# A 2D-DFT mixing layer and a SoLU feed-forward layer: even and odd halves shared between two frequencies, and the transposition of u by 32 x 32 blocks and moves

## The chip, the cores and the metric

The kernel runs on one core of a Trainium2 chip, in one launch. The metric is the device time of that launch in microseconds (us); the kernel before takes 2172.12 us, the median of 3 runs (2170.49 to 2173.72). The engines are called by the names of the profile: PE (matrix multiply), PEld (its weight loads), DVE (vector), ACT (scalar, activation functions), POOL (GpSimd), SP (which issues transfers), and the 16 DMA engines.

## What is computed

The reference takes x of 8 batches x 3136 rows x 256 features and does two layers:

```python
X = np.fft.fft(np.fft.fft(x, axis=1), axis=2).real      # (8, 3136, 256)
h = X.reshape(25088, 256) @ w_in                        # (25088, 1024)
e = np.exp(h - h.max(-1)); sm = e / (e.sum(-1) + 1e-9)
solu = h * sm
ln = (solu - mean(solu)) / np.sqrt(var(solu) + 1e-6) * g_ln
out = ln @ w_out                                        # (25088, 256)
```

All data are float32 to the kernel, except that the weights can come as float64 words, which it narrows itself.

## The kernel before

**First part, the transform over the sequence.** The 3136 positions are 49 x 64. Batches are taken in four pairs. `load` brings in rows and their mirror rows, `fold` adds x[n, d] and x[-n, -d] on POOL (L121) and forms sums and differences over the features on DVE (L112, L113), `transform1` sums over 49 with matmuls (L148), ACT evicts (L151), the result goes through DRAM (`zd`) and `turn` brings it back with another index on the partitions. `transform2` (L166) sums over 64. Only 25 of the 49 residues k1 are computed: for each k1 the product gives the "+" frequency, and with the sign of half of the features changed the "-" frequency. The feature transform is folded into w_in beforehand, so it costs nothing per token.

**Second part.** For each pair, k1 and sign there is one tile of 128 tokens, 4 x 49 = 196 tiles in all. On a tile:

- `up_half`, twice: h, a 128 x 1024 tile in PSUM, from two 128 x 128 stationary blocks of q (or qm, its copy with the changed sign, made at L176) against `Wi` (L190).
- `solu`: the maximum of h (L195, DVE), the exponential with its sum (L198, ACT), u = h * e with its sum (L200, DVE), the mean on POOL (L203), the centred square with its sum (L206, ACT), and five small POOL operations for the reciprocal root.
- `transpose`: eight PE transposes of u (L224) into PSUM, evicted half by ACT (L230) and half by DVE (L228).
- `down`: eight matmuls of 128 x 256 (L235) against `Wo`, scaled by DVE (L237) and stored. The layer norm's scale and mean lie in `Wo`.

**Order.** The program's order is written out by hand: for tile i, the first half of up(i), transpose(i-1), the second half of up(i), solu(i), then (on a "+" tile) transform2 of the next k1 and one step of the next pair's first part, and last down(i-1). `ahead` spreads a pair's first part over the 25 steps of the pair before it; the first pair's runs alone at the start, followed by the preparation of the weights. The PSUM pools are `ps_h` (2 tiles of 2 banks), `ps_t` (2 banks) and `ps_m` (2 banks, shared by the results of transform1, transform2 and down).

Of the kernel before, what the change touches and what calls it, by code (L numbers as in the profile page):

```python
# [10 lines left out]
I32 = mybir.dt.int32  # L11
ALU = mybir.AluOpType
# [5 lines left out]
# The sequence index is n = N2 * n1 + n2 and its frequency k = k1 + N1 * k2.  # L18
# The frequencies k1 of 0..NK-1 are computed; k1 and N1 - k1 share their products.
# [5 lines left out]
CH = 8  # L25
NC = NH // CH

# The layout of the 256 folded features: cosine part at 0..128, sine part (1..127) at 129..255.
# [4 lines left out]
def kernel(  # L33
# [13 lines left out]
    """Sequence DFT with even and odd folds, feature DFT folded into w_in, then SoLU and its layer norm.  # L47

    With U the cosine transform over the sequence of x folded evenly in the features, and V the sine
    transform of x folded oddly, the real part of the 2D DFT is U C - V S at frequency k and U C + V S  # L50
    at -k. So h = [U, V] @ [C w_in; -S w_in], and for -k the features of V change their sign.
    """
# [10 lines left out]
    out_b = out.rearrange("(b s) d -> b s d", b=B)  # L63
# [4 lines left out]
    gpool = ctx.enter_context(tc.tile_pool(name="gpool", bufs=2))  # L68
    qpool = ctx.enter_context(tc.tile_pool(name="qpool", bufs=3))
    small = ctx.enter_context(tc.tile_pool(name="small", bufs=4))  # L70
    dram = ctx.enter_context(tc.tile_pool(name="dram", bufs=2, space=bass.MemoryType.DRAM))
    ps_h = ctx.enter_context(tc.tile_pool(name="ps_h", bufs=2, space=PSUM))
    ps_t = ctx.enter_context(tc.tile_pool(name="ps_t", bufs=2, space=PSUM))
    ps_m = ctx.enter_context(tc.tile_pool(name="ps_m", bufs=2, space=PSUM))

    F = const.tile([PR, 6, ZR], FP32, name="F")
    T = const.tile([P, NK, P], FP32, name="T")
    Wi = const.tile([P, KD, FF], FP32, name="Wi")
    Wo = const.tile([P, KF, D], FP32, name="Wo")
    ident = const.tile([P, P], FP32, name="ident")  # L80
    ones = const.tile([P, P], FP32, name="ones")
    neg_half = const.tile([P, 1], FP32, name="neg_half")
    idx = const.tile([PR, NP * NC], I32, name="idx")
    sg = const.tile([P, 1], FP32, name="sg")

# [1 line left out]

    class Pair:
        def __init__(self, p):
            self.p = p  # L90
            self.raw, self.y, self.y0 = {}, {}, None
            self.g = None

    def load(pr, c):
        """Rows n2 = 8c + 1 .. 8c + 8, and those of S - n beside them (in descending order of n2)."""
        r = slice(pr.p * PR, (pr.p + 1) * PR)
        xa = xpool.tile([PR, CH, D], FP32, tag="xa", name="xa")
        xb = xpool.tile([PR, CH, D], FP32, tag="xb", name="xb")
        nc.sync.dma_start(out=xa, in_=x_pn[r, c * CH + 1 : (c + 1) * CH + 1, :])
        i = pr.p * NC + c  # L100
        nc.gpsimd.indirect_dma_start(
            out=xb.rearrange("p l d -> p (l d)"), out_offset=None, in_=x_g,
            in_offset=bass.IndirectOffsetOnAxis(ap=idx[:, i : i + 1], axis=0))
        x0 = None
        if c == NC - 1:
            x0 = xpool.tile([PR, 1, D], FP32, tag="x0", name="x0", bufs=1)
            nc.sync.dma_start(out=x0, in_=x_pn[r, 0:1, :])
        pr.raw[c] = (xa, xb, x0)

    def fold_features(o, i):  # L110
# [3 lines left out]
        nc.vector.tensor_copy(out=o[:, :, 0:129:128], in_=i[:, :, 0:129:128])  # L114

    def fold(pr, c):
        """x[n, d] + x[-n, -d], then its even and odd parts in d. Rows n2 = 0 and 32 hold their own mirrors."""
        xa, xb, x0 = pr.raw.pop(c)
        n = CH - 1 if c == NC - 1 else CH
        a, rb = xa[:, 0:n, :], xb[:, ::-1, :][:, 0:n, :]  # L120
        nc.gpsimd.tensor_tensor(out=a[:, :, 1:D], in0=a[:, :, 1:D], in1=rb[:, :, D - 1 : 0 : -1], op=ALU.add)  # L121
        nc.gpsimd.tensor_tensor(out=a[:, :, 0:1], in0=a[:, :, 0:1], in1=rb[:, :, 0:1], op=ALU.add)
        y = xpool.tile([PR, CH, D], FP32, tag="y", name="y")
        fold_features(y, xa)
        pr.y[c] = y
        if c == NC - 1:
            pr.y0 = xpool.tile([PR, 1, D], FP32, tag="y0", name="y0", bufs=1)
            fold_features(pr.y0, x0)

    def transform1(pr, s):  # L130
        """Sum over n1 for rows n2 = 2s + 1, 2s + 2; out: (b, cosine or sine, k1) on partitions.

        The last row holds n2 = 0, of no sine part, in its cosine part and n2 = 32 in its sine part."""
# [3 lines left out]
        if l == 0:  # L137
            pr.z = zpool.tile([ZR, CH, D], FP32, tag="z", name="z")
# [13 lines left out]
        if l == CH - 2:  # L152
            nc.sync.dma_start(out=pr.zd[:, c * CH : (c + 1) * CH, :], in_=pr.z)

    def turn(pr):
        """(b, cosine or sine, n2) onto partitions."""
        pr.g = gpool.tile([P, NK, D], FP32, tag="g", name="g")
        for j in range(4):
            nc.sync.dma_start(out=pr.g[j * NH : (j + 1) * NH, :, :],
                              in_=pr.zd[j * NK : (j + 1) * NK, :, :].rearrange("k n d -> n k d"))  # L160

    def transform2(pr, k1):
        """Sum over n2 for both batches; out: folded features on partitions, tokens (b, k2) free."""
        ps = ps_m.tile([P, KD, P], FP32, tag="m", name="ps2")
        for h in range(KD):
            nc.tensor.matmul(ps[:, h, :], pr.g[:, k1, h * P : (h + 1) * P], T[:, k1, :],  # L166
                             start=(h == 0), stop=(h == KD - 1), skip_group_check=True)
        q = {"+": qpool.tile([P, KD, P], FP32, tag="q", name="q")}
        nc.vector.tensor_copy(out=q["+"], in_=ps)  # L169
        if k1:  # L170
            # -(k1 + 49 k2) is (49 - k1) + 49 (63 - k2): the negative frequencies run backwards.
            q["-"] = qpool.tile([P, KD, P], FP32, tag="qm", name="qm")
            for h in range(KD):
                o = q["-"][:, h, :].rearrange("p (b k) -> p b k", b=2)
                i = ps[:, h, :].rearrange("p (b k) -> p b k", b=2)[:, :, ::-1]
                nc.scalar.activation(out=o, in_=i, func=ACT.Copy, scale=sg if h else 1.0)  # L176
        return q

# [1 line left out]

    class Tokens:
        def __init__(self, p, k1, s):
            self.p, self.k1, self.s = p, k1, s

    def up_half(t, half):
        if half == 0:
            t.h = ps_h.tile([P, FF], FP32, tag="h", name="h")
        fs = slice(half * HW, (half + 1) * HW)
        for h in range(KD):
            nc.tensor.matmul(t.h[:, fs], t.q[:, h, :], Wi[:, h, fs], start=(h == 0), stop=(h == KD - 1))  # L190

    def solu(t):
        """u = h exp(h - max h), its sum and centred sum of squares, and the sum of the exponentials."""
        nmax = small.tile([P, 1], FP32, tag="nmax", name="nmax")
        nc.vector.tensor_reduce(out=nmax, in_=t.h, axis=AX.X, op=ALU.max, negate=True)  # L195
        t.u = fpool.tile([P, FF], FP32, tag="u", name="u")
        esum = small.tile([P, 1], FP32, tag="esum", name="esum")
        nc.scalar.activation(out=t.u, in_=t.h, func=ACT.Exp, bias=nmax, accum_out=esum)  # L198
        usum = small.tile([P, 1], FP32, tag="usum", name="usum")
        nc.vector.scalar_tensor_tensor(out=t.u, in0=t.h, scalar=1.0, in1=t.u, op0=ALU.mult, op1=ALU.mult,  # L200
                                       accum_out=usum)
        nmean = small.tile([P, 1], FP32, tag="nmean", name="nmean")
        nc.gpsimd.tensor_scalar(out=nmean, in0=usum, scalar1=-1.0 / FF, scalar2=None, op0=ALU.mult)  # L203
        sq = fpool.tile([P, FF], FP32, tag="sq", name="sq", bufs=1)
        ssq = small.tile([P, 1], FP32, tag="ssq", name="ssq")
        nc.scalar.activation(out=sq, in_=t.u, func=ACT.Square, bias=nmean, accum_out=ssq)  # L206
        # 1 / (sum * sqrt(var(u / sum) + 1e-6)) = (var(u) + 1e-6 sum^2) ** -0.5
        es = small.tile([P, 1], FP32, tag="es", name="es")
        nc.gpsimd.tensor_scalar(out=es, in0=esum, scalar1=1e-9, scalar2=1e-3, op0=ALU.add, op1=ALU.mult)
        es2 = small.tile([P, 1], FP32, tag="es2", name="es2")  # L210
        nc.gpsimd.tensor_tensor(out=es2, in0=es, in1=es, op=ALU.mult)
        v = small.tile([P, 1], FP32, tag="v", name="v")
        nc.gpsimd.tensor_scalar(out=v, in0=ssq, scalar1=1.0 / FF, scalar2=es2, op0=ALU.mult, op1=ALU.add)  # L213
# [237 lines left out]
```

## Time and profile before

| | busy us | share of the span |
|---|---|---|
| PE | 1788.7 | 83% |
| PEld | 1238.2 | 57% |
| DVE | 846.8 | 39% |
| ACT | 670.6 | 31% |
| POOL | 382.0 | 18% |

The profiled span is 2166.9 us with 19414 instructions; the mean granted clock of the PE is 0.903. A float32 matmul leaves two records: the 196 tiles x 4 matmuls of L190 are 1568 records. The ends of PE records are modelled, so durations of PE work are best read as differences between starts. The transfers average 39 GB/s over the span.

### The profile page before, as it was taken

To read this page: it belongs to the slowest core of one execution; us is meant where nothing else is said; L and a number is where in the kernel's file an instruction comes from. 1 tells how busy PE (TensorE), PEld (TensorE's weight loads), DVE (VectorE), ACT (ScalarE), POOL (GpSimd) and SP (SyncE) were. 2 spreads that over 40 slices of the span, in tenths; PEclk is the share of its full clock that TensorE was granted. 3 is DMA by queue.
4 is the path that set the end of the run, shared out by engine and by line. 5 is a ranking of instruction groups with operands and counts; after the bars stand their busy time and mean duration, and the time that the engine had idled before them with its cause. 6 is when DMAs were issued, how large, how long until landed. Compare 5 with 4: busy or idle time off the path is not lost. (4 is left out here: it accounts for less than half of the span.)

```text
span 2166.9 us, 19414 instructions
## 1 busy us (share of the span) xinstructions
PE 1788.7 (83%) x6992; PEld 1238.2 (57%) x6992; DVE 846.8 (39%) x1327; ACT 670.6 (31%) x1240; POOL 382.0 (18%) x1034
## 2 busy tenths in 40 slices
PE   2357888788799878878879987887887999999998
PEld 1135555555566555555556755555555666777666
DVE  2853233323334323332433433333233344444444
ACT  1113223223333322332332323233233234434443
POOL 3002121212112212121211221212121111111111
PEclk8679899889899888888999988889899899999999
DMA  9511010001042101000104210101010400000000
GB/s 240 133 33 42 24 46 13 25 13 28 10 90 75 42 20 50 12 26 12 28 11 88 77 42 16 54 10 28 11 29 11 88 18 18 17 16 18 18 18 17
DMA packets 56783, 84.78 MB, mean 39 GB/s; under 512 B 12038, under 2 KB 50574, under 8 KB 51696
## 3 DMA queue, kind: packets, MB, share of 16 engines
q1 hardware_dynamic: 48528, 65.19, 12.7%
q0 software_dynamic: 2048, 12.85, 2.1%
q10 hardware_dynamic: 6112, 5.52, 1.3%
q8 instruction: 55, 0.90, 0.2%
q14 instruction: 40, 0.33, 0.1%
HBM read 44.72 MB, written 38.80 MB: 39 GB/s over the span
## 5 line engine op out<-in xcount | busy, mean ns | idle before, releaser
L235 PE MATMUL ps_o<-Wo,uT 128*128 128x256 f32 x3136 | 833.5, 425 | 270.8 <-ACT qm L176 215.9
L235 PEld LDWEIGHTS ps_o<-Wo,uT 128*128 128x128 f32 x3136 | 668.7, 217 | 444.7 <-ACT qm L176 235.5
L198 ACT ACTIVATE u<-h,nmax 128x1024 f32<-128x1024 f32 x196 | 218.4, 1114 | 634.3 <-DVE nmax L195 634.3
L190 PE MATMUL h<-Wi,q 128*128 128x512 f32 x800 | 384.4, 604 | 7.8 <-DVE q L169 7.8
L190 PE MATMUL h<-Wi,qm 128*128 128x512 f32 x768 | 361.1, 592 | 0.0
L200 DVE SCALAR_TENSOR_TENSOR u<-h,u 128x1024 f32<-128x1024 f32 x196 | 240.0, 1225 | 249.4 <-ACT u L198 249.4
L206 ACT ACTIVATE sq<-u,nmean 128x1024 f32<-128x1024 f32 x196 | 225.1, 1148 | 317.7 <-POOL nmean L203 317.7
L195 DVE TENSOR_REDUCE nmax<-h 128x1 f32<-128x1024 f32 x196 | 239.9, 1224 | 193.5 <-PE h L190 193.5
L203 POOL TENSOR_SCALAR nmean<-usum 128x1 f32<-128x1 f32 x196 | 45.7, 233 | 1515.3 <-DVE u L200 1515.3
L228 DVE COPY uT<-tp 128x512 f32<-128x512 f32 x196 | 135.5, 691 | 372.3 <-PE tp L224 372.3
L230 ACT COPY uT<-tp 128x512 f32<-128x512 f32 x196 | 114.9, 586 | 415.9 <-PE tp L224 415.9
L224 PEld LDWEIGHTS tp<-ident,u 128*128 128x128 f32 x1568 | 183.5, 141 | 104.5 <-issue 103.7
L237 DVE TENSOR_SCALAR ot<-ps_o,rs 128x256 f32<-128x256 f32 x196 | 94.0, 480 | 369.4 <-issue 364.3
L190 PEld LDWEIGHTS h<-Wi,q 128*128 128x128 f32 x800 | 147.5, 195 | 115.4 <-issue 103.7
L224 PE MATMUL tp<-ident,u 128*128 128x128 f32 x1568 | 203.2, 273 | 0.5 <-DVE u L200 0.5
L190 PEld LDWEIGHTS h<-Wi,qm 128*128 128x128 f32 x768 | 138.4, 190 | 96.8 <-issue 91.8
L215 POOL TENSOR_TENSOR rs<-v,neg_half 128x1 f32<-128x1 f32 x196 | 113.2, 578 | 16.3
L148 PE MATMUL ps<-y,F 98*100 98x258 f32 (+3 forms) x288 | 71.5, 385 | 43.3 <-DVE y L114 43.3
L166 PEld LDWEIGHTS ps<-T,g 128*128 128x128 f32 x400 | 60.4, 191 | 47.4 <-issue 47.4
L213 POOL TENSOR_SCALAR v<-ssq,es 128x1 f32<-128x1 f32 x196 | 52.4, 267 | 177.6 <-ACT sq L206 175.5
L148 PEld LDWEIGHTS ps<-y,F 98*100 98x100 f32 x288 | 45.5, 178 | 54.7 <-DVE y L114 30.4
L121 POOL TENSOR_TENSOR xa<-xa,xb 98x2040 f32<-98x2040 f32 (+1 forms) x16 | 70.1, 4379 | 28.9 <-DMA xa<-in_x_dram 16.2
(50 smaller groups left out, 544.4 us busy)
## 6 DMA issues: line engine op xcount, KB each, us to landing
out_dram<-ot SPq DMA_DIRECT2D x392, 64.0 KB
zd<-z SPq DMA_DIRECT2D x16, 800.0 KB
g<-zd SPq DMA_DIRECT2D x16, 800.0 KB
xa<-in_x_dram SPq DMA_DIRECT2D x16, 784.0 KB
raw_in_moe_w_in_dram<-in_moe_w_in_dram ACTq DMA_DIRECT2D x1, 2048.0 KB
raw_in_moe_w_out_dram<-in_moe_w_out_dram ACTq DMA_DIRECT2D x1, 2048.0 KB
T<-in_t_tab_dram ACTq DMA_DIRECT2D x2, 400.0 KB
x<-in_x_dram SPq DMA_DIRECT2D x4, 98.0 KB
```

Source lines behind the costliest of these rows:

```text
L148: nc.tensor.matmul(o[..., cs], F[:, 2 * t + h, :], i[..., cs], start=first, stop=True, skip_group_check=True)
L190: nc.tensor.matmul(t.h[:, fs], t.q[:, h, :], Wi[:, h, fs], start=(h == 0), stop=(h == KD - 1))
L195: nc.vector.tensor_reduce(out=nmax, in_=t.h, axis=AX.X, op=ALU.max, negate=True)
L198: nc.scalar.activation(out=t.u, in_=t.h, func=ACT.Exp, bias=nmax, accum_out=esum)
L200: nc.vector.scalar_tensor_tensor(out=t.u, in0=t.h, scalar=1.0, in1=t.u, op0=ALU.mult, op1=ALU.mult, accum_out=usum)
L206: nc.scalar.activation(out=sq, in_=t.u, func=ACT.Square, bias=nmean, accum_out=ssq)
L215: nc.gpsimd.tensor_tensor(out=t.rs, in0=v, in1=neg_half, op=ALU.pow)
L224: nc.tensor.matmul(tp[:, c, :], t.u[:, f * P : (f + 1) * P], ident, is_transpose=True, start=(c == 0), stop=(c == n - 1), skip_group_check ...
L228: nc.vector.tensor_copy(out=o, in_=tp)
L230: nc.scalar.copy(o, tp)
L235: nc.tensor.matmul(ps, t.uT[:, c, :], Wo[:, c, :], start=(c == 0), stop=(c == KF - 1))
L237: nc.vector.tensor_scalar(out=ot, in0=ps, scalar1=t.rs, scalar2=None, op0=ALU.mult)
```

## The change

Nearly everything but the mathematics of the first part is rewritten.

1. **Even and odd parts.** The first 128 folded features make an even part of h, the other 128 an odd part; h of "+" is their sum and h of "-" their difference. The two products are made once for both signs. `Wi` has a factor -2 on the weights (from `narrow_in`), so that the joins only add: h0 = -0.5 * (even + odd), h1 = h0 + odd. One cosine feature (the 129th) doesn't fit into the even half; it comes in as an outer product on DVE in `even`, from the row `w_mid` and a column `t.r` that `spread` brings across partitions with a small transfer.
2. **Joins that also give the maximum.** `join` is a `tensor_tensor_reduce` on DVE for each sign, which writes h to SBUF and accumulates its maximum; the tile's separate maximum (L195) is gone. ACT negates the maximum.
3. **Squares.** The bias is the sum of u, with the scale -1024, in place of the mean made on POOL; the statistics take the factor 1024 ** -3.
4. **Moved blocks.** The transposition of u is a DVE transpose of 32 x 32 blocks for each sign, which interleaves both signs in 8-byte steps, and then 16 transfers SBUF to SBUF for each two units (2 x k1) that put the blocks onto their partitions, in runs of 64 values. The first four units still go through PE transposes. `down` follows four units later, with a stationary operand of step 2.
5. **Around it.** Scaling the output is on ACT; "-" rows are stored by an indirect transfer; PSUM is now two tiles of 2 banks (`h0`, `h1`, one of each) and four banks for the rest; the first part works in chunks of 4 rows (not 8), its DRAM round trip in groups of 5 k1; the weights' preparation is shorter and interleaved with the first pair's transform, in place of following it.

The core of the diff, with new code for the second part (L numbers are those before):

```diff
-    def up_half(t, half):
-            nc.tensor.matmul(t.h[:, fs], t.q[:, h, :], Wi[:, h, fs], start=(h == 0), stop=(h == KD - 1))
+    def up(t, c):
+        ps = ps_h.tile([P, FF], FP32, tag=f"h{c}", name=f"ps_h{c}")
+        for half in range(2):
+            fs = slice(half * HW, (half + 1) * HW)
+            nc.tensor.matmul(ps[:, fs], t.q[:, c * P : (c + 1) * P], Wi[:, c, fs], start=True, stop=True)
+        return ps
+    def even(t, ps):
+        nc.vector.scalar_tensor_tensor(out=t.ev, in0=w_mid, scalar=t.r, in1=ps,
+                                       op0=ALU.mult, op1=ALU.add)
-        nc.vector.tensor_reduce(out=nmax, in_=t.h, axis=AX.X, op=ALU.max, negate=True)
+    def join(t, ps):
+        for s in t.signs:
+            t.h[s] = fpool.tile([P, FF], FP32, tag="h", name="h", bufs=2)
+            nc.vector.tensor_tensor_reduce(out=t.h[s], in0=t.h[0] if s else t.ev, in1=ps,
+                                           scale=1.0 if s else -0.5, scalar=-3.0e38, op0=ALU.add, op1=ALU.max,
+                                           accum_out=t.nmax[:, s : s + 1])
-        nc.gpsimd.tensor_scalar(out=nmean, in0=usum, scalar1=-1.0 / FF, scalar2=None, op0=ALU.mult)
-        nc.scalar.activation(out=sq, in_=t.u, func=ACT.Square, bias=nmean, accum_out=ssq)
+    def square(t, s):
+        nc.scalar.activation(out=t.h[s], in_=t.u[s], func=ACT.Square, bias=t.usum[:, s : s + 1], scale=-float(FF),
+                             accum_out=t.ssq[:, s : s + 1])
-    def transpose(t):
+    def turn_blocks(t, s):
+        for o in (s,) if len(t.signs) == 2 else (0, 1):
+            nc.vector.transpose(out=t.batch.v[:, t.w, :, o], in_=t.u[s])
+    def move_blocks(batch, units, engines=(nc.sync,)):
+        v = batch.v[:, units].rearrange("p w (c q n) s -> p q (w c) (n s)", q=4, n=32)
+        uT = batch.uT[:, units].rearrange("p w c i m -> p i (w c) m")
+        for i in range(4):
+            for q in range(4):
+                a, b = slice(32 * i, 32 * i + 32), slice(32 * q, 32 * q + 32)
+                engines[i % len(engines)].dma_start(out=uT[b, i], in_=v[a, q])
-            nc.tensor.matmul(ps, t.uT[:, c, :], Wo[:, c, :], start=(c == 0), stop=(c == KF - 1))
-        nc.vector.tensor_scalar(out=ot, in0=ps, scalar1=t.rs, scalar2=None, op0=ALU.mult)
+            nc.tensor.matmul(ps, uT[:, c, :, s], Wo[:, c, :], start=(c == 0), stop=(c == KF - 1))
+        nc.scalar.mul(out=t.ot[s], in_=ps, mul=t.rs[:, s : s + 1])
```

and the order of the main loop after the change, for unit i, from the fifth unit on (`lag` is 4, `old` is unit i - 4):

```python
store(units[i - lag - 1])
begin(i)        # even(cur, up(cur, 0)); cur.odd = up(cur, 1); transform2, take2 and spread of unit i + 2
join(cur, cur.odd)
expo(cur)
ahead_pe(ahd, cur.k1)                     # transform1 of the next pair, turn
ps_o = [down(old, s) for s in order]
for s in cur.signs: product(cur, s)
for s in cur.signs: square(cur, s); turn_blocks(cur, s)
scale(old, order[0], ps_o[0])
if cur.w: move_blocks(batches[-1], slice(0, 2))       # after each second unit
stats(cur)
ahead(ahd, cur.k1)                        # add_mirror (POOL), fold (DVE), loads of the next pair
scale(old, order[1], ps_o[1])
```

## The prediction, written before the result was known

> **What bounds the kernel now.** I read the stretches of busy time first, then the timeline of one stretch, then the waits, then the groups of instructions, and last the transfers. The stretches show a PE that is the bound wherever nothing blocks it: with the last pair (no first part beside it) it is busy all the time at full clock, while DVE, ACT and POOL stay under half.
>
> ```profile
> core 0: us, PE busy (x) PEld busy (x) DVE busy (x) ACT busy (x) POOL busy (x), PEclk, DMA share, GB/s
> 0.00:140.00 140.00, 41.88 (x113) 24.16 (x114) 85.67 (x203) 13.07 (x20) 24.40 (x18) 0.74 0.60 145
> ...
> 1000.00:1120.00 120.00, 97.45 (x370) 67.56 (x370) 40.69 (x62) 34.33 (x64) 18.74 (x52) 0.90 0.07 18
> ...
> 1840.00:1960.00 120.00, 120.00 (x514) 84.37 (x513) 55.84 (x83) 48.84 (x92) 22.39 (x76) 1.00 0.08 17
> ```
>
> The reader is to see three stages: 140 us of preparation with little PE work, the long stage with 81% of PE at clock 0.90, and the last with 100% at 1.00. The PE timeline of the last stage prices each part by differences of starts:
>
> ```profile
> 1857.55 0.61 PE L166 MATMUL ps<-T,g 128*128 128x128 f32 x4
> 1857.99 3.62 PE L235 MATMUL ps_o<-Wo,uT 128*128 128x256 f32 x16
> 1861.44 1.88 PE L190 MATMUL h<-Wi,qm 128*128 128x512 f32 x4
> 1863.16 1.04 PE L224 MATMUL tp<-ident,u 128*128 128x128 f32 x8
> 1864.04 1.88 PE L190 MATMUL h<-Wi,qm 128*128 128x512 f32 x4
> 1865.75 3.62 PE L235 MATMUL ps_o<-Wo,uT 128*128 128x256 f32 x16
> ```
>
> Per tile: half an up is 1863.16 - 1861.44 = 1.72 us, so up 3.43; transposes 0.88; down 3.45; transform2 0.44 for two tiles. Two tiles: 2 x 7.76 + 0.44 = 15.96, and the measured period is 16.0. The middle stage loses its time in one wait:
>
> ```profile
> PEld ps_o L235 <- ACT qm L176: 235.5, 48, 5.0
> PE ps_o L235 <- ACT qm L176: 215.9, 48, 4.5
> ```
>
> 48 times down waits for a `ps_m` bank that ACT has yet to empty, 4.5 us each, and after it the clock is low: at 904.34 that down takes 5.99 us, not 3.62. Last, the rows that price the new vector work:
>
> ```profile
> L200 DVE SCALAR_TENSOR_TENSOR u<-h,u 128x1024 f32<-128x1024 f32 x196 | 240.0, 1225 | 249.4 <-ACT u L198 249.4
> L206 ACT ACTIVATE sq<-u,nmean 128x1024 f32<-128x1024 f32 x196 | 225.1, 1148 | 317.7 <-POOL nmean L203 317.7
> L112 DVE TENSOR_TENSOR y<-xa 98x1016 f32<-98x1016 f32 x16 | 19.5, 1218 | 122.2 <-POOL xa L121 122.2
> L281 DVE SCALAR_TENSOR_TENSOR rest<-ex,rest 128x512 f32<-128x512 int32 x4 | 2.8, 693 | 0.1
> ```
>
> One pass over 1024 float32 values costs 1.22 us on DVE, with one input in PSUM (L200) or both in SBUF (L112), and 1.15 us on ACT.
>
> **What the Trainium skill says.** (1) "VectorE: DVE Perf Modes", the section on the TRN2 errata, prices a float32 two-input pass at (N + 151) / 0.96 ns, 1224 ns at N = 1024; L200's 1225 agrees. (2) "Vector Engine (DVE) Microarchitecture Reference", section 3.8, says the 32 x 32 transpose sustains one element per cycle per lane; no run here shows one. Its section 7 says that a scalar_tensor_tensor with two non-bf16 SBUF sources runs at half the rate; L281 has two such sources and takes 693 ns for 512, formula 691, so the trace disagrees, though without an accumulator. (3) "DMA: Bandwidth & Descriptors", section Bandwidth, says small descriptors are slow with HBM only and not SBUF to SBUF; this trace has no SBUF-to-SBUF transfer. (4) "SBUF — State Buffer", section on the two sides, says a vector instruction with two SBUF inputs contends with a POOL instruction that reads SBUF; no wait in this trace proves it.
>
> **The change part by part, per unit (one k1, two tiles).**
>
> *Up.* Four matmuls of 128 x 512 in place of eight: 3.43 us of PE, 3.43 saved.
>
> *PE transposes.* 2 x 0.88 = 1.76 us of PE leave, with two evictions of 0.59 (ACT) and two of 0.69 (DVE).
>
> *Down and transform2* stay: 2 x 3.45 + 0.44 = 7.34. The step of 2 in the stationary operand should cost nothing: weight loads (190 ns) lie beside matmuls 216 ns apart; at twice the time it would show.
>
> PE sum: 3.43 + 7.34 = 10.77 us, with the 0.04 of overhead above 10.8, against 16.0. One unit per pair has one sign (3.45 less). Transform1 is 16 steps of 1.03 us a pair (from the timeline), 16.5 us for each of three pairs.
>
> *DVE.* even, two joins, two products, two block transposes: 7 x 1.22, and four accumulator reads of 0.08: 8.9 us. Folds: eight chunks a pair of two passes over 508 values, (508 + 151) / 0.96 = 0.69 each, together 11 us a pair, 0.45 a unit. product waits 0.3 us for the first exponential. About 9.3 to 9.7, under PE's 10.8 to 11.5, so I count it as hidden. The join with an accumulated maximum is taken as L200.
>
> *ACT.* take2 0.37, two negations of 0.2, two exponentials and two squares of 1.15 + 0.19, two scalings of 0.45, the z copies 16 x 0.59 / 25 = 0.4: 7.4 us, hidden under PE.
>
> *POOL.* The mean (0.23 each) goes, and with it the hop between product and square; it held neither DVE nor PE. Five statistics for both signs together 1.5, the indirect store 1.4, half-chunk add_mirror 2.3 every second unit: under 5 us.
>
> *The wait of 4.5 us.* `ps_m` has four banks and down's results leave on ACT; a bank comes round after four tiles, by which time it was emptied an iteration ago. I count all 48 waits as removed, with the low clock behind them.
>
> *The moves.* Each batch of two units moves 128 x 4096 values = 2.1 MB in 8192 runs of 256 B. The nearest row is the load of T, also runs of 256 B, but from HBM. Its best and its poor microsecond:
>
> ```profile
> DMA packets 560, 0.18 MB, mean 179 GB/s; under 512 B 539, under 2 KB 539, under 8 KB 560
> ```
>
> ```profile
> DMA packets 382, 0.12 MB, mean 122 GB/s; under 512 B 379, under 2 KB 379, under 8 KB 379
> ```
>
> 8192 / 539 = 15.2 us, 8192 / 379 = 21.6 us a batch. By (3) I take the fast end, or better: 15. Other traffic a pair: 6.4 MB of x at the 280 GB/s of the start (23 us), zd 11, g at the 194 GB/s measured after 70 us (17), output at 1.9 us per 393 KB (30): 81 us over 12.5 batches, 6.5 each. Sum 21.5 us in a PE period of 2 x 11.5 = 23: hidden, barely. In time: the batch starts at the end of its odd unit and is needed about 2.4 iterations, 26 us, later. Sixteen issues lie in SP's queue, at 1.15 us for 800 runs as g shows (4.61 for four), so 0.7 each, 12 us a batch; behind them wait the stores, `spread` (needed by even two units on) and the loads of x (three units of lead), which all bear 12 to 16 us.
>
> *Start.* Before, transform2 began at 132.5 us. Afterwards 10.9 MB (x 6.4, both weights 4.1, tables) at 280 GB/s take 39 us; the last fold, transform1, the DRAM round trip for two k1 and spread add some 20: 60 us. In the first four units PE has no down and waits for DVE and ACT, about 5 us each: 20. *End.* The last scaling and store: 6.
>
> **Sum of the forecast.** 100 x 10.8 - 4 x 3.45 + 49.5 + 8 (the first units' PE transposes and the column mean) = 1124; + 60 + 20 + 6 = 1210; measured time exceeds the span by 5 us now: 1215. For DVE meeting POOL's SBUF reads (add_mirror 2.3 us) and moves that come late now and then I add 4% of the main part, 45 us: 1260.
>
> **The rivals.**
>
> *Moves set the pace.* If SBUF runs go at 379 per us, a batch takes 21.6 + 6.5 = 28.1 us in the first three pairs and 24 in the last: 35.5 x 28.1 + 12.5 x 24 = 1298, with start, first units and end some 140: 1440. For: only 1.5 us of reserve at the fast rate, and one queue for everything. Against: the skill's (3), and that T's slow microseconds are reads from HBM.
>
> *DVE sets the pace.* If product runs at half rate (skill, section 7) or the block transpose with its 8-byte steps does, a unit has 11.1 us, 11.5 with the wait, 12.5 with folds and POOL: 75 x 12.5 + 25 x 11.5 = 1225, + 90: 1315. For: DVE has only 1 to 2 us of slack. Against: L281.
>
> *Slower than before.* In one microsecond (34 to 35) only 188 runs of T landed beside 33 of w_out's: 8192 / 188 = 43.6, with 6.5 50 us a batch, 48 x 50 + 130 = 2530. For: that microsecond. Against: it has twice as many bytes of another load in it.
>
> **How the numbers follow.** Forecast 0.60, moves 0.20, DVE 0.15, slower 0.03, a mixture of late moves and low clock 0.02. The predicted time is the forecast's, 1260. No case goes under 1195 (no stalls, a start of 45 us), so low is 1190; the slow moves and DVE cases reach 1440, and a cost between T's two rates and worse 1480, leaving out 2 in 10. Faster: the first three and half of the mixture, 0.96; slower 0.03; same the other half of the mixture, 0.01.
>
> **What would show it.** Right: PE over 90% busy at clock near 1.0 in the middle, about 22 to 23.5 us per two units, no wait of down on ACT, block transposes near 1.2 us, main loop starting near 60 us. Moves: down waits for uT, DMA share near 1, PE clock under 0.9. DVE: up waits for a join, DVE over 95% busy. Start: transform2 much later than 60 us. Wrong altogether: a batch's moves over 45 us.

## The result and the profile after

The kernel after takes 1190.16 us (median of 4 runs, 1188.86 to 1191.12), beside 2171.3 us for the kernel before on the same chip: a ratio of 0.5479 [0.5471, 0.5487]. The direction, the bound and the order of size came as forecast; the time lies 70 us under the forecast of 1260 us, at the low end of the range. The stretches of busy time of the kernel after, in stages of 180 us after the start, stand for the three stages shown of before:

```profile
core 0: us, PE busy (x) PEld busy (x) DVE busy (x) ACT busy (x) POOL busy (x), PEclk, DMA share, GB/s
0.00:57.00 57.00, 31.76 (x96) 19.19 (x97) 43.37 (x89) 25.74 (x40) 11.99 (x18) 1.00 0.84 223
57.00:120.00 63.00, 55.90 (x238) 37.94 (x237) 54.38 (x78) 42.47 (x86) 25.19 (x40) 1.00 0.45 106
120.00:300.00 180.00, 180.00 (x747) 137.81 (x746) 140.07 (x188) 105.95 (x227) 91.48 (x131) 1.00 0.86 176
...
840.00:1020.00 180.00, 180.00 (x733) 136.98 (x732) 141.71 (x184) 105.72 (x215) 72.31 (x121) 1.00 0.70 144
```

From 120 to 1020 us PE is busy in all of every stretch, at the full clock, where the middle stage of before had 97.45 of 120 us at 0.90. DVE now works 78% of the time, and the DMA engines 70 to 86%; neither stops PE. What is left of PE's waits is short (us in total, times, longest):

```profile
PE ps L171 <- DVE y L124: 25.2, 4, 20.8
PE ps_h L227 <- DVE ev L233: 3.0, 1, 3.0
PE ps_h L227 <- DVE nmax L241: 1.6, 2, 0.8
PE ps_o L325 <- ACT uT L310: 0.9, 1, 0.9
...
PE ps_o L325 <- ACT ot L330: 0.5, 1, 0.5
```

The first line is the start, while PE waits for the first folded rows. The rest happens seven times, among the first units and at the end: after the start the list has 7.4 us in all, against 270 us of PE's waits in L235 before. The timeline of PE in the last pair (start, duration, instructions) gives the price of a unit by differences of starts, as before:

```profile
902.23 3.60 PE L227 MATMUL ps_h<-Wi,q 128*128 128x512 f32 x8
905.67 0.61 PE L199 MATMUL ps<-T,g 128*128 128x128 f32 x4
906.11 7.08 PE L325 MATMUL ps_o<-Wo,uT 128*128 128x256 f32 x32
913.03 2.31 PE L227 MATMUL ps_h<-Wi,q 128*128 128x512 f32 x5
```

Up for both signs 3.44, transform2 0.44, two downs 6.92: a unit of 10.80 us, forecast 10.8. In the earlier pairs a unit with a step of transform1 is 11.65 us, so that step is 0.86. The groups of instructions of the kernel after, for the new vector work (mean ns after the busy time):

```profile
L272 POOL TENSOR_SCALAR es<-esum 128x2 f32<-128x2 f32 (+1 forms) x100 | 116.4, 1164 | 425.3 <-ACT u L251 425.1
L258 DVE SCALAR_TENSOR_TENSOR u<-h,u 128x1024 f32<-128x1024 f32 x196 | 239.9, 1225 | 33.5 <-ACT u L251 20.7
L293 DVE STREAM_TRANSPOSE v<-u 128x1024 f32<-128x1024 f32 x192 | 227.5, 1224 | 0.1
L241 DVE CUSTOM_DVE_ANT_0 h<-ev,ps_h 128x1024 f32<-128x1024 f32 x100 | 122.1, 1221 | 48.9 <-PE ps_h L227 45.3
```

Joins, products and block transposes each take one pass, 1.22 us; the product's two inputs are now both in SBUF and its time is what it was. The 1164 ns of a POOL operation on 128 x 2 values is strange, and comes back below.

### The profile page after: what moved, and what is told of

Its sections match the earlier page's. It is cut to its first block, busy times and chain, and to the rows that moved or that the text cites. A ratio compares the mean times of both kernels' runs of the same rounds, so it can differ in the third digit from the quotient of the medians.

```text
span 1189.0 us, 15738 instructions
## 1 busy us (share of the span) xinstructions
PE 1152.6 (97%) x4720; PEld 874.5 (74%) x4720; DVE 912.3 (77%) x1234; ACT 679.9 (57%) x1404; POOL 505.9 (43%) x766
## 4 chain that ended last, share of the span: by engine, by line
PE 93%; DMA 3%; DVE 2%; SPq 1%; issue 1%; POOL 1%; ACT 0%; DVEq 0%; ACTq 0%; POOLq 0%
PE ps_o L325 56%; PE ps_h L227 28%; PE ps L171 5%; PE ps L199 4%; DMA raw_in<-in_moe_w_in_dram 2%; PE wps L456 1%; DMA r<-q 1%; SPq L179 1%; DVE h L241 0%; POOL uT L319 0%; DMA out_dram<-ot,idx 0%; DVE y L123 0%; SPq L442 0%; PE ps_t L305 0%; DVE xa L131 0%
## 5 line engine op out<-in xcount | busy, mean ns | idle before, releaser
L325 PE MATMUL ps_o<-Wo,uT 128*128 128x256 f32 x3136 | 693.4, 379 | 1.3 <-ACT uT L310 0.9
L227 PE MATMUL ps_h<-Wi,q 128*128 128x512 f32 x800 | 360.5, 593 | 5.1 <-DVE ev L233 3.0
L272 POOL TENSOR_SCALAR es<-esum 128x2 f32<-128x2 f32 (+1 forms) x100 | 116.4, 1164 | 425.3 <-ACT u L251 425.1
L227 PEld LDWEIGHTS ps_h<-Wi,q 128*128 128x128 f32 x800 | 151.5, 190 | 154.3 <-issue 142.3
L265 ACT ACTIVATE h<-u,usum 128x1024 f32<-128x1024 f32 x196 | 224.5, 1147 | 14.8 <-DVE u L258 9.0
L233 DVE SCALAR_TENSOR_TENSOR ev<-w_mid,r,ps_h 128x1024 f32<-128x1024 f32 x100 | 127.8, 1278 | 135.0 <-PE ps_h L227 127.1
L251 ACT ACTIVATE u<-h,neg 128x1024 f32<-128x1024 f32 x196 | 225.6, 1151 | 6.4
L293 DVE STREAM_TRANSPOSE v<-u 128x1024 f32<-128x1024 f32 x192 | 227.5, 1224 | 0.1
L241 DVE CUSTOM_DVE_ANT_0 h<-ev,ps_h 128x1024 f32<-128x1024 f32 x100 | 122.1, 1221 | 48.9 <-PE ps_h L227 45.3
L241 DVE CUSTOM_DVE_ANT_0 h<-h,ps_h 128x1024 f32<-128x1024 f32 x96 | 117.3, 1222 | 14.2 <-ACT neg L249 0.5
L249 ACT ACTIVATE neg<-nmax 128x1 f32<-128x1 f32 x196 | 38.8, 198 | 71.0 <-DVE nmax L241 70.9
```

The source lines that it names most:

```text
L227: nc.tensor.matmul(ps[:, fs], t.q[:, c * P : (c + 1) * P], Wi[:, c, fs], start=True, stop=True)
L233: nc.vector.scalar_tensor_tensor(out=t.ev, in0=w_mid, scalar=t.r, in1=ps, op0=ALU.mult, op1=ALU.add)
L241: nc.vector.tensor_tensor_reduce(out=t.h[s], in0=t.h[0] if s else t.ev, in1=ps, scale=1.0 if s else -0.5, scalar=-3.0e38, op0=ALU.add, op1 ...
L251: nc.scalar.activation(out=t.u[s], in_=t.h[s], func=ACT.Exp, bias=t.neg[:, s : s + 1], accum_out=t.esum[:, s : s + 1])
L265: nc.scalar.activation(out=t.h[s], in_=t.u[s], func=ACT.Square, bias=t.usum[:, s : s + 1], scale=-float(FF), accum_out=t.ssq[:, s : s + 1])
L272: nc.gpsimd.tensor_scalar(out=es[:, n], in0=t.esum[:, n], scalar1=1e-9, scalar2=1e-3, op0=ALU.add, op1=ALU.mult)
```

## The experiments

Two questions were left. The change does several things at once, so what of the 981 us belongs to which? And the forecast had put 70 us too much: how near are DVE, POOL and the moves to hurting, since it allowed 45 us for them? In what follows "before" and "after" are the two kernels, and a time without an interval is one run.

**1. The waits alone.** The kernel before, with transform2 and the copies of its result ahead of the activation functions:

```diff
             if cur:
                 up_half(cur, 1)
-                solu(cur)
                 if cur.s == "+":
                     ...
                         qs[units[n]] = transform2(pairs[units[n][0]], units[n][1])
-                    if cur.p + 1 < NP:
-                        ahead(pairs[cur.p + 1], cur.k1)
+                solu(cur)
+                if cur.s == "+" and cur.p + 1 < NP:
+                    ahead(pairs[cur.p + 1], cur.k1)
```

> The kernel before, with transform2 and its three copies (DVE q, ACT qm) emitted ahead of solu instead of behind it; same work. If the 48 waits of 4.5 us on the bank that ACT empties, and the low clock behind each (about 2.5 us), are a real part of the gain: 48 x 7 = 336 us less, 1836 us, wait of down on qm gone, clock near 1.0. Rival: the wait only moves to another engine (DVE or ACT become late by the copies), and the time stays within 60 us of 2172.

Measured: 1873.05 us, 298 less than before. What PE waits for on the `uT` evictions, first in the kernel before, then in this run, and below it what is left of the `qm` waits:

```profile
PE ps_o L235 <- DVE uT L228: 54.0, 12, 4.5
```

```profile
PE ps_o L235 <- DVE uT L228: 63.2, 12, 5.3
...
PE ps_o L235 <- ACT qm L176: 9.8, 45, 0.2
```

The wait for the `qm` copies, 215.9 us before, is 9.8: the copies had stood behind an exponential and a square on ACT, and both gaps and low clock came from that order. The saving falls 37 us short of the expectation: the `qm` waits still take 9.8, another wait grew by 9.2, and the remaining 18 are not traced; the price of 2.5 us for the low clock behind each wait was an estimate. That other wait, of down for the eviction of `uT` on DVE, I had passed over in the list of before.

**2. The second wait as well.** The run of experiment 1, with POOL's addition of the mirrored rows one step before the fold that needs it, as the kernel after has it:

```diff
-    def fold(pr, c):
-        xa, xb, x0 = pr.raw.pop(c)
+    def add_mirror(pr, c):
+        xa, xb, _ = pr.raw[c]
...
+    def fold(pr, c):
+        xa, xb, x0 = pr.raw.pop(c)
...
+        elif step % 5 == 1 and step // 5 < NC:
+            add_mirror(pr, step // 5)
...
```

> The kernel before with the copies and transform2 of a unit emitted ahead of its solu (as in the run with the copies first, 1873 us) and, besides, GpSimd's add of the mirrored part of u emitted one step before the fold that needs it. Theory: the 12 waits of TensorE for the folded u that were left there (63 us, 5.3 us each) come from that add, which stands in front of the fold; they go, and so does what is left of the low clock: 1790 us (1770 to 1815). Rival: the add only moves its time to another wait (GpSimd's means late, so the squares and the banks): within 20 us of 1873, with the 63 us under another releaser.

Measured: 1780.55 us, 92.5 less again. The stretches of this run:

```profile
300.00:700.00 400.00, 396.72 (x1687) 276.17 (x1686) 187.45 (x277) 162.29 (x299) 98.89 (x249) 1.00 0.20 49
```

PE is at 99%, clock 1.00, and the 63 us have left the list of waits. DVE's own wait shows why, first in experiment 1, then here:

```profile
DVE y L112 <- POOL xa L121: 126.0, 15, 19.4
```

```profile
DVE y L112 <- POOL xa L120: 39.5, 3, 18.6
```

Twelve waits at the fold have gone. There DVE had stood, waiting for POOL's 4.4 us addition, with the eviction of `uT` queued behind it. Two changes of order that add no operation and take none away are worth 391 us, 40% of the whole gain.

**3. PE's work.** The kernel after, with every matmul of up issued twice, the same result written both times; this puts the 3.43 us a unit back that the sharing between the two signs took out.

```diff
-            nc.tensor.matmul(ps[:, fs], t.q[:, c * P : (c + 1) * P], Wi[:, c, fs], start=True, stop=True)
+            for _ in range(2):
+                nc.tensor.matmul(ps[:, fs], t.q[:, c * P : (c + 1) * P], Wi[:, c, fs], start=True, stop=True)
```

> The kernel after, with each up matmul issued twice into the same place (same result, 3.43 us of PE more per unit, as without the shared even and odd parts). If PE sets the pace alone: 1190 + 100 x 3.43 = 1533 us, PE at 97% or more. Rival: if something else (moves, DVE) set the pace, part of the 343 us would be hidden: under 1480.

Measured: 1523.85 us, 334 more for some 343 us of PE work. PE sets the pace in the kernel after, nearly microsecond for microsecond.

**4. PE transposes in place of the moves.** The kernel after, with all units on the path that it has for its first four, and one buffer moved from `v` to `uT` to hold them:

```diff
-                self.v = fpool.tile([P, 2, FF, 2], FP32, tag="v", name="v32", bufs=2)
-            self.uT = fpool.tile([P, 2, KF, 4, 64], FP32, tag="uT", name="uT", bufs=2)
+                self.v = fpool.tile([P, 2, FF, 2], FP32, tag="v", name="v32", bufs=1)
+            self.uT = fpool.tile([P, 2, KF, 4, 64], FP32, tag="uT", name="uT", bufs=3)
...
-        whole = 4
+        whole = len(units)
```

> The kernel after, with every unit transposed on PE as the first four are, no moves and no block transposes (a third uT buffer, one v buffer). If PE sets the pace: 96 units x 1.76 us = 169 us more, 1359 us. Rival: the four transposed tiles go through the same four PSUM banks as down and the evictions (two of 0.62 on ACT, two of 0.69 on DVE) make PE wait: above 1420 us with idle time on PE. If the moves were the bound: less than 1190.

Measured: 1484.93 us; the rival was right. PE waits in this run:

```profile
PE ps_t L305 <- ACT ot L330: 75.5, 90, 0.9
```

A transpose needs a PSUM bank which ACT gives back by scaling the old output, and in this order the scaling stands behind the next unit's first square. A period in the last pair is 13.92 us, where 10.79 and two transposes of 0.88 make 12.55. To see whether that wait is the whole of the excess, the scaling was moved ahead:

```diff
+                if i < whole and old:
+                    for s, ps in zip(order, ps_o):
+                        scale(old, s, ps)
...
                     begin(i + 1)
...
-            if old:
+            if old and not cur:
                 scale(old, order[0], ps_o[0])
...
-            if old and 1 in old.signs:
+            if old and not cur and 1 in old.signs:
                 scale(old, order[1], ps_o[1])
```

> The kernel after with all transposes of u on TensorE (no moves), as in the run that took 1485 us, but with ScalarE's scaling of the old output's tiles emitted ahead of the next unit's first square, so that it no longer stands behind it. Theory: the waits of TensorE for a PSUM bank that the scaling gives back (75.5 us in 90 units, and as much before weight loads) go, and TensorE alone sets the period of 12.55 us a unit: 1365 us (1350 to 1385). Rival: the wait moves to another bank or to the squares, 1450 or more.

Measured: 1415.68 us, between the two expectations. The wait for the scaling is gone, and a smaller one came, for the evictions:

```profile
PE ps L171 <- ACT uT L310: 19.3, 46, 0.6
PE ps_o L325 <- ACT uT L310: 17.2, 46, 0.9
```

The period is 13.17 us. So the moves are worth 225 us in the better of two orders: 169 of these are PE's transposes (96 units x 1.76), the other 56 go to waits that this order has and a better one might not (0.62 us a unit in the last pair). Whether a third order reaches 12.55 was not tried.

**5. How near the moves are.** The kernel after, with the two signs kept apart instead of interleaved, so that the same bytes move in twice as many runs, of 128 bytes (the shapes of `v` and `uT`, and the slices that `down` reads, follow):

```diff
-            nc.vector.transpose(out=t.batch.v[:, t.w, :, o], in_=t.u[s])
+            nc.vector.transpose(out=t.batch.v[:, t.w, o, :], in_=t.u[s])
...
-        v = batch.v[:, units].rearrange("p w (c q n) s -> p q (w c) (n s)", q=4, n=32)
+        v = batch.v[:, units].rearrange("p w s (c q n) -> p q (w s c) n", q=4, n=32)
```

> The kernel after without the interleaving of the two signs: same bytes moved, in 16384 runs of 128 B per batch in place of 8192 of 256 B; down reads step 1, block transposes write step 1. Theory that the cost is by run (16 issues took 13.2 us for 8192 runs, 1.6 ns each): 26 us of issue a batch and some 3 of the queue's other work, 29 us against PE's 21.6 to 23.3, so moves set the pace: 48 x 29 + 130 = 1520 us. Rival, by bytes: 1190 us. A strided stationary operand or strided block writes that cost something would show as shorter weight loads or block transposes here.

Measured: 1220.7 us, 300 us under the theory that the cost is by run and 31 above the rival by bytes. The transfers between 905 and 927 us, first of the kernel after, then of this run (q1 is the queue of the moves: packets, MB, share of the 16 engines' time):

```profile
DMA packets 9046, 2.63 MB, mean 119 GB/s; under 512 B 8724, under 2 KB 8980, under 8 KB 9044
...
q1 hardware_dynamic: 8948, 2.34, 46.1%
```

```profile
DMA packets 19160, 3.51 MB, mean 159 GB/s; under 512 B 18646, under 2 KB 18902, under 8 KB 19158
...
q1 hardware_dynamic: 18806, 2.56, 89.6%
```

0.461 x 16 x 22 us / 8948 is at most 18.1 ns of an engine for a run of 256 bytes; in the second window it is at most 0.896 x 352 / 18806 = 16.8 ns for 128 bytes. (At most, since the times of packets overlap: the shares of the second window's queues add up to 108%.) So the DMA engines' cost is much more by the run than by the byte. What the theory had wrong is the term that it took for the bound, the issue on SP: sixteen issues of twice the runs take 15.6 to 17.1 us there, not 26. A batch of the last pair of the kernel after costs the DMA engines 8192 x 18.1 / 16 = 9.3 us of its 21.6. Twice the runs just fit there: between 920 and 1120 us of this run the DMA share is 0.87, and PE is busy all the time. In the earlier pairs, where loads and the DRAM round trip are added, the share is 1.00 to 1.03, and there it hurts: DVE waits for the small transfer of `spread`, queued behind the moves (7.7 us in the kernel after), in this run:

```profile
DVE ev L233 <- DMA r<-q: 106.5, 24, 10.1
```

PE waits 9.6 us for the moves themselves, in two places, and the run is 31 us longer in the end. The Trainium skill's "DMA: Bandwidth & Descriptors", section "Why small descriptors are slow (HBM only)", says that transfers between SBUF and SBUF don't suffer their penalty. These runs disagree for this shape: at 17 to 18 ns a run at most, 128 bytes move at about half the rate of 256.

**6. How near DVE is.** The kernel after, with one more pass of DVE a unit, or two (the sum of u with itself, written over the even part and not used):

```diff
                 for s in cur.signs:
                     ...
                     if i >= whole:
                         turn_blocks(cur, s)
+                        if s >= 1:
+                            nc.vector.tensor_tensor(out=cur.ev, in0=cur.u[s], in1=cur.u[s], op=ALU.add)
```

> The kernel after with one more DVE pass over 128 x 1024 (1.22 us, result unused) behind the second block transpose of 93 units: 113 us of DVE. Theory that PE alone sets the pace and DVE has about 2 us a unit to spare: 1190 to 1196 us. Rival, the forecast's allowance that DVE is close enough to hold PE up now and then: 30 us or more on top, 1220 us.

Measured: 1192.44 us, ratio 0.5492 [0.5484, 0.5499] beside 0.5479 [0.5471, 0.5487] for the kernel after. DVE's 107 us of added work (1019.8 busy, 912.3 in the kernel after) cost 2 us between the medians, and the intervals overlap. With `s >= 0`, two passes:

> Two such passes a unit (189 in all, 231 us of DVE). DVE then has 8.85 + 2.44 = 11.3 us a unit, 11.7 to 12.1 with folds and the wait for the exponential, against PE's 10.8 to 11.65: DVE sets the pace, about 0.5 us a unit in the last pair and 0.6 in the others, 1190 + 58 = 1248 us (1210 to 1290), up waits for a join. If it stays under 1200, DVE had more to spare than I count.

Measured: 1243.43 us, ratio 0.5729 [0.572, 0.5738]. The waits of ACT for the maximum (70.9 us in the kernel after), and a stretch, in this run:

```profile
ACT neg L249 <- DVE nmax L241: 331.8, 98, 6.0
```

```profile
300.00:600.00 300.00, 293.51 (x1189) 222.76 (x1189) 280.88 (x348) 165.10 (x353) 167.37 (x200) 0.99 0.70 157
```

DVE is at 94% and now holds PE up: PE waits 10.3 us for joins, as expected, and 16.6 for folds. The first of the two passes is all but free, and of the second, 108 us of work (1127.5 busy), 51 us come out as time. So I estimate DVE's slack in the kernel after at one and a half passes a unit, some 1.7 us, within the 1 to 2 that the prediction gave it.

**7. The two new pieces of arithmetic.** The mean on POOL again as the squares' bias:

```diff
-        nc.scalar.activation(out=t.h[s], in_=t.u[s], func=ACT.Square, bias=t.usum[:, s : s + 1], scale=-float(FF),
+        nmean = small.tile([P, 1], FP32, tag="nmean", name="nmean")
+        nc.gpsimd.tensor_scalar(out=nmean, in0=t.usum[:, s : s + 1], scalar1=-1.0 / FF, scalar2=None, op0=ALU.mult)
+        nc.scalar.activation(out=t.h[s], in_=t.u[s], func=ACT.Square, bias=nmean,
...
-        nc.gpsimd.tensor_scalar(out=v[:, n], in0=t.ssq[:, n], scalar1=float(FF) ** -3, scalar2=None, op0=ALU.mult)
+        nc.gpsimd.tensor_scalar(out=v[:, n], in0=t.ssq[:, n], scalar1=1.0 / FF, scalar2=None, op0=ALU.mult)
```

> The kernel after with the mean of u made on POOL again (one 128x1 operation a tile) and taken as the bias of the squares, scale 1. Theory: ACT has 3 us or more a unit to spare, so the hop costs nothing: 1190 us within 3. Rival: POOL's queue (statistics that wait for the squares, add_mirror of 2.3 us in front) delays squares, the ACT queue holds up the scalings and take2 behind them, and PE waits for a bank: 1200 us or more, in the first three pairs only.

Measured: 1187.6 us, ratio 0.5472 [0.5464, 0.548]. And the joins without the factor -2:

```diff
-            narrow(w, raw, [(o[:, j : j + n], -(2.0 ** -19))], self.units.pop(0))
+            narrow(w, raw, [(o[:, j : j + n], 2.0 ** -20)], self.units.pop(0))
...
-            nc.vector.tensor_tensor_reduce(out=t.h[s], in0=t.h[0] if s else t.ev, in1=ps,
-                                           scale=1.0 if s else -0.5, scalar=-3.0e38, op0=ALU.add, op1=ALU.max,
+            nc.vector.tensor_tensor_reduce(out=t.h[s], in0=t.ev, in1=ps,
+                                           scale=1.0, scalar=-3.0e38, op0=ALU.subtract if s else ALU.add, op1=ALU.max,
```

> The kernel after without the factor -2 on the weights: both joins read the even part, the first adds and the second subtracts the odd part. The output is meant to be the same. Theory: the join is one pass of VectorE over 1024 values whatever its operation, about 1.22 us each, with VectorE at 77% of the span and TensorE the bound, so 1190 us (within 3) and a ratio of 0.548; one less step in the chain from the first join to the second changes nothing, since VectorE runs them in order anyway. Rival: the subtraction costs more than the addition (a second pass, or a slower form); at twice 1.22 us for 96 joins VectorE would be at some 1030 of 1190 us, which the run with one more pass a unit showed to cost 2 us or less, but the mean duration of the second join in the trace would be 2.4 us.

Measured: 1188.65 us, ratio 0.5474 [0.5466, 0.5483]; the mean join takes 1219 ns, 1221 in the kernel after. Both intervals overlap that of the kernel after. These two pieces of arithmetic make no difference in time that the runs can tell: one shortens a chain under a PE that is busy anyway, the other swaps one pass for an equal one.

**8. The start.** The kernel after, with a chunk of x and its fold ahead of each quarter of w_in, to give PE its first work sooner (the core of the edit):

```diff
-            weights.piece_in(c)
-            if c:
-                load(first, c - 1, rooms.get(c - 1))
+            load(first, c, rooms.get(c))
...
+            weights.piece_in(c)
```

> The kernel after with the start in another order: each chunk of x is asked for ahead of a quarter of w_in, and folded ahead of that quarter's narrowing. Same work. Now PE first runs at 20.8 us and the first up at 58.9 us. Theory: PE starts near 13 us and the first up moves by 3 to 6 us, and the whole time by the same: 1185 us. Rival: the start is bound by the transfers (10.9 MB, busy until 48 us) or by DVE, and nothing moves: 1190 us.

Measured: 1192.21 us, ratio 0.5493 [0.5485, 0.55]; the first up at 60.50 us, not 58.88. PE began at 16 us, not 20.8, but then waited for folded rows in three other places (3.2, 1.7 and 4.3 us). In the profiled run the granted clock was also 0.82 in the first 57 us, where the kernel after has 1.00, so the two starts can't be compared to the microsecond; but none of its five runs is under 1190.8 us. This other order gains nothing; what bounds the start is left open.

## What the prediction had right, and which step of it failed

**The account of what was gained, 981 us.**

| part | us | from |
|---|---|---|
| waits of down for the copies of `qm`, with the low clock | 298 | experiment 1 |
| waits for the fold behind POOL's addition | 92 | experiment 2 |
| up once for both signs | 334 | experiment 3 |
| PE's transposes | 169 | 96 x 1.76, by the trace; experiment 4 gives 225 with waits of its own order |
| start: first transform2 at 57.34, before 132.5 | 75 | the two timelines |
| sum | 968 | |

The 13 us left are not traced, and what made the start shorter was not tested by an edit. The parts were measured on two different kernels, so their sum needn't close better than that.

**The account of what was forecast too much, 70 us.** From the first transform2 at 57.34 us to the last PE record's end at 1185.40 are 1128.1 us. PE's work in it, by the measured steps, is 100 x 10.8 - 13.8 + 48 x 0.86 + 9.6 (7 tiles of PE transposes and the column mean) = 1117.1, so 11.0 are left for waits and what follows them; PE's list names 7.4. The differences below add up to -69.5, the rest is rounding.

| term of the forecast | forecast | measured | difference |
|---|---|---|---|
| start | 60 | 57.3 | -2.7 |
| unit on PE | 10.8 | 10.8 | 0 |
| transform1, 48 steps | 49.5 | 41.3 | -8.2 |
| PE transposes of the first units, column mean | 8 | 9.6 | +1.6 |
| idle PE among the first units (measured: from 57.34 us to the end) | 20 | 11.0 | -9.0 |
| allowance for DVE meeting POOL and for late moves | 45 | 0 | -45 |
| end | 6 | 3.6 | -2.4 |
| measured time above the span (1190.16 is the median; the profiled run has 2.1) | 5 | 1.2 | -3.8 |

The step that failed is the last term of the sum: "For DVE meeting POOL's SBUF reads (add_mirror 2.3 us) and moves that come late now and then I add 4% of the main part, 45 us". The bound and the sum of PE's work were right; this term was given 45 us and measured nothing: PE's stretches from 120 to 1020 us show no idle time at all, and the 11.0 us above are all that the rest has. I had added it to the likeliest case, on a slack of DVE that I myself had worked out as positive; it belonged into the range. Next come the first units, 20 us of waits for at most 11.0, and transform1, whose step was priced by a record's duration, 1.03, whose end is modelled, and not by the difference of starts, 0.86. The start came out near the forecast by luck: the transfers kept the DMA engines busy to 48 us, not 39 (share 0.90 in the 4 us before, 0.15 in the 4 us after), and transform2 began 9 us later, not 20. Nearly all terms erred upwards, and the low end had no room for that. It doesn't follow from the prediction's own terms either: without stalls and with a start of 45 us they give 1124 + 45 + 6 + 5 = 1180, or 1200 with the first units' 20, but not 1195.

Both halves of the allowance fall for a reason that the runs show:

- *Moves that come late.* The forecast priced a run by the load of T, 15 us a batch; the engines need 9.3 in the last pair. Between 300 and 900 us, with loads beside, the trace's packets of 256 bytes take 22.3 ns on the mean, 11.4 us a batch. The sixteen issues of a batch take 13.2 us of SP in the last pair, forecast 12. No wait for a move stands in PE's list of the kernel after, and twice the runs cost 31 us only. The rival "moves set the pace" took T's slow rate, 21.6 us a batch, for that of the runs; why T had been slower, the runs don't show.
- *DVE meeting POOL.* The 24 long additions of `add_mirror` (L131), which the forecast had named, never lie beside a product in the trace of the kernel after. What meets the product is a small operation, and it is POOL that waits. The timeline of DVE and POOL there (start, duration):

```profile
910.01 1.23 DVE L258 SCALAR_TENSOR_TENSOR u<-h,u 128x1024 f32<-128x1024 f32 x1
910.08 1.22 POOL L272 TENSOR_SCALAR es<-esum 128x2 f32<-128x2 f32 x1 [5.76 <-ACT u L251]
...
911.37 0.20 POOL L275 TENSOR_TENSOR es<-es 128x2 f32<-128x2 f32 x1
```

The product, with two inputs in SBUF, starts 0.07 us earlier; POOL's operation on two values a row, 193 ns in experiment 7, lasts to its end. In the kernel after all 196 products take 1212 to 1230 ns: none was drawn out. This is a matter of the order. In the run with PE transposes and the scaling first, POOL's addition starts first, and DVE pays:

```profile
585.31 2.35 POOL L131 TENSOR_TENSOR xa<-xa,xb 98x1020 f32<-98x1020 f32 x1
586.34 2.40 DVE L258 SCALAR_TENSOR_TENSOR u<-h,u 128x1024 f32<-128x1024 f32 x1
587.62 1.18 POOL L132 TENSOR_TENSOR xa<-xa,xb 98x4 f32<-98x4 f32 x1
```

The product takes 2.40 us and ends 1.08 us after the addition, which ends at 587.66; POOL's next addition, of 4 values, then lasts 1.18. In this run 22 of the 24 additions meet a product so, and each of these products ends 1.08 to 1.09 us after its addition. The trace of before held one such case already, of a copy on DVE, of which the prediction said that no wait in it proves the point:

```profile
25.69 4.58 POOL L121 TENSOR_TENSOR xa<-xa,xb 98x2040 f32<-98x2040 f32 x1
...
25.83 4.48 DVE L114 COPY y<-xa 98x16 f32<-98x16 f32 x1
```

That copy takes 0.18 us as a rule. For the products, this agrees with what the Trainium skill's "SBUF — State Buffer", section "SBUF: two separate sides", states: whichever of a DVE operation with two SBUF inputs and a POOL operation that reads SBUF starts first has the port for its whole length, and the other blocks. I had read the page as a tax on DVE. It matters who is first, and who has time: POOL, busy for 43% of the span, has.

**The rest, point by point.** The 48 waits on ACT and the low clock behind them went, as forecast; the 12 waits behind the fold went too, which I had not listed among what is removed. The rival "DVE sets the pace" rested on half the rate for a product with two SBUF inputs (the Trainium skill's "Vector Engine (DVE) Microarchitecture Reference", section 7) or for the block transposes; both take 1.22 us, the product with its accumulator, so here too the trace disagrees with that section. The stationary operand of step 2 cost 196 ns a weight load on the mean in the kernel after, 193 with step 1 in experiment 5, beside matmul records 216 ns apart: hidden. The mean on POOL held nobody, as forecast (experiment 7).

## What to carry to other kernels

Add up the work of the engine that will be the bound, by differences of starts, and leave it at that: what might go wrong besides belongs into the range, and slack that comes out positive is not charged for (here 107 us more of DVE's work cost 2). Before a design is replaced, read the whole list of waits of the old one and ask of each what stands ahead of the releaser in its queue; two changes of order gave 40% of what the new design gave. Where DVE reads two SBUF operands beside POOL, look at which starts first, since in these traces that one was not slowed and the other lost the overlap.

## What the runs showed of the hardware

- An SBUF to SBUF run costs a DMA engine 18.1 ns at 256 bytes and 16.8 ns at 128, each the time of the packets over their number, so at most that. The figure moves with what else goes on: in the run with the mean on POOL the same 256-byte runs took 15.8 ns (39.7% of the 16 engines for 24115 packets between 1040 and 1100 us); why is not traced. Sixteen issues of 512 runs took SP 13.2 to 16.1 us, of 1024 runs 15.6 to 17.1: the issue goes by the instruction far more than by the runs.
- POOL's operation on 128 x 2 values takes 1164 ns on the mean in the kernel after and 193 in the run with the mean on POOL. There the mean's own operation goes first and seems to take part of the wait: 420 ns on the mean, 233 in the kernel before.
- A transpose of 128 x 1024 float32 values in 32 x 32 blocks takes DVE 1224 ns with its output in steps of 8 bytes, and 1221 closed up (experiment 5).
